# One packed input array for the first loads, and the first two chunks' transposed columns in one transfer each

## The chip, the core and the metric

The kernel runs on one core of a Trainium2 chip. The core has a matrix engine (TensorE, PE in the profile), a vector engine (VectorE, DVE), an activation engine (ScalarE, ACT), a general engine (GpSimd, POOL) and a queue engine (SyncE, SP). PE multiplies from on-chip memory into accumulators; 16 DMA engines bring data from device memory. Each engine works through its own queue in order and waits for others by semaphores. The metric is the time of one execution on the device, in microseconds.

## The reference

Inputs are `x` (1, 2048, 448), `wqkv` (448, 1344), `wo` (448, 448), a gate vector, and the parameters of a state space convolution (448 channels, 256 states). Cut to what matters:

```python
g = sigmoid((x * gate_w).sum(-1, keepdims=True))
# a: linear attention, 16 heads of 28
q, k, v = split_heads(x @ wqkv)
phi = lambda t: where(t > 0, t + 1, exp(t)) + 1e-6
pq, pk = phi(q), phi(k)
kv = einsum("bhsd,bhse->bhde", pk, v);  z = einsum("bhsd->bhd", pk)
num = einsum("bhqd,bhde->bhqe", pq, kv)
den = einsum("bhqd,bhd->bhq", pq, z)[..., None] + 1e-6
a = merge_heads(num / den) @ wo
# b: convolution of x with K over the sequence
P = exp((A * dt[:, None])[:, :, None] * arange(L))
K = 2 * einsum("dn,dnl->dl", C, P).real
b = irfft(rfft(x, 2 * L) * rfft(K, 2 * L))[:L] + x * D_skip
return g * a + (1 - g) * b
```

## The kernel before

The 2048 rows of `x` are cut into 16 chunks of 128. In device memory one array, `xin`, holds for every chunk 128 rows of 1024 numbers (4096 bytes): first 512 numbers of the chunk transposed (four blocks of 128 columns; constants `EV` = 384 and `NAT` = 512 mark the last block's beginning and the end), then 448 in natural order and 64 of them again (`XC` = 1024). The weights for K, Q and V are arrays of 128 partitions by four slices of 448 or 450 columns (`wk_d`, `wq_d`, `wv_d`); a row of one slice is 1792 or 1800 bytes, and rows of one slice lie 7168 or 7200 bytes apart.

Products are made in three parts. Each operand is rounded to a high part (names ending in `h`) and the rest (ending in `l`); PE adds high times high, low times high and high times low. For the x chunks and weight slices at the start, ACT makes the high part (`ACT.copy`, lines 279 and 292) and DVE subtracts (line 269). Only GpSimd makes both parts of the last Q slice.

The order of all work is written out by hand: engines run their queues in program order. At the start chunks 0 and 1 are done together, slice by slice (`pair`, line 561): for K the slices 3, 1, 2, 0, then for Q the same. Slice 3 uses the chunks' columns 384 to 512, the others columns 0 to 384. A slice needs six products of K (two chunks, three parts; the last slice four). The eight K and Q weight slices land in a corner of the output buffer `y` that is free at that time (`wkr`, `wqr`), so the profile shows their loads as `y<-in`; the loads of the chunks are `xr<-in`. Before the first product PE runs eight warm-up products (line 300).

All loads of the start are issued by SP, but for the K slice 3, which ACT issues. They use eight semaphores in turn, so each load waits until the one eight places ahead has landed.

After the two chunks' K and Q, PE goes on with the sums of x-transposed times K features (`do_g`, line 495), then chunk by chunk with K and Q projections (line 396), the convolution's triangular products (line 511), and at the end with transposes of Q features (line 783) and the last product (line 805). Behind the main part stands a branch for a general convolution (`general_conv`), which these inputs don't take.

Of the kernel before, what the change touches and what calls it, by code (L numbers as in the profile page):

```python
# [15 lines left out]
P = 128  # L16
S = 2048
D = 448
# [6 lines left out]
NAT = 4 * P  # L25
LO = NAT + D
XC = LO + 64
# [13 lines left out]
EV = 3 * P  # L41
# [135 lines left out]
            SP.dma_start(out=byc(out, c - ZB + 1), in_=yb)  # L177

@with_exitstack
def gated_mix_kernel(ctx: ExitStack, tc: tile.TileContext, xin, wk_d, wq_d, wv_d, wo_d, abc_d, ldt_d, dsk_d,  # L180
                     tri_d, ident_d, mask_d, gcat_d, sel_d, nabc_d, nldt_d, xrev_d, lag_d, out):
    nc = tc.nc
    PE, ACT, DVE, POOL, SP = nc.tensor, nc.scalar, nc.vector, nc.gpsimd, nc.sync

# [46 lines left out]
    xr, xh, xl = {}, {}, {}  # L231

    def load_x(c):
        xr[c] = pf[:, 4 * D:4 * D + XC] if c == 3 else xp.tile([P, XC], F32, name="xr", tag="xr")
        if c > 1:
            SP.dma_start(out=xr[c], in_=xin[c])

    def load_part(c, lo, hi):
        SP.dma_start(out=xr[c][:, lo:hi], in_=xin[c, :, lo:hi])

    S0 = NC * D - 4 * J * N
    wkr = yf[:, S0:S0 + J * D].rearrange("p (j d) -> p j d", j=J)
    wqr = yf[:, S0 + J * D:S0 + J * (2 * D + 2)].rearrange("p (j d) -> p j d", j=J)
    abc = pf[:DJ, 3 * J * N:7 * J * N].rearrange("p (i j n) -> p i j n", i=4, j=J)
    load_x(0)
    load_x(1)
    for eng, j in ((ACT, 3), (SP, 1), (SP, 2), (SP, 0)):
        if j == 3:
            load_part(0, EV, NAT)
        elif j:  # L250
            load_part(j - 1, 0, EV)
        eng.dma_start(out=wkr[:, j], in_=wk_d[:, j])
        if j == 3:
            load_part(1, EV, NAT)
    for j in (3, 1, 2, 0):
        SP.dma_start(out=wqr[:, j], in_=wq_d[:, j])
    load_part(0, NAT, XC)
    load_part(1, NAT, XC)
    load_x(2)
    SP.dma_start(out=dsk, in_=dsk_d.to_broadcast([P, D]))  # L260
    load_x(3)
# [6 lines left out]
    def low(eng, o, r, h):  # L268
        eng.tensor_tensor(out=o, in0=r, in1=h.bitcast(F32), op=ALU.subtract)  # L269
# [8 lines left out]
    def split_part(c, lo, hi):  # L278
        ACT.copy(xh[c][:, lo:hi], xr[c][:, lo:hi])
        low(DVE, xl[c][:, lo:hi], xr[c][:, lo:hi], xh[c][:, lo:hi])  # L280
# [10 lines left out]
    def high_w(eng, h, r, j):  # L291
        (ACT.copy if eng is ACT else eng.tensor_copy)(h[:, j], r[:, j])

    def low_w(eng, h, l, r, j):
        p = slice(0 if j else 64, P)
        low(eng, (l if j else h)[p, j], r[p, j], h[p, j])
# [256 lines left out]
    def pair(wh, wl, n, tags):  # L553
        o = [ps.tile([P, 512], F32, name=t, tag=t) for t in tags]

        def run(j, parts, last=False):
            xk = slice(j * P, (j + 1) * P)
            for c in range(2):
                for p in parts:
                    a = (xl if p == 1 else xh)[c][:, xk]  # L560
                    PE.matmul(o[c][:, :n], lhsT=a, rhs=(wl if p == 2 else wh)[:, j], start=(j, p) == (3, 0),  # L561
                              stop=last and p == parts[-1])
        return o, run
# [5 lines left out]
    low_w(DVE, wkh, wkl, wkr, 3)  # L569
    split_part(1, EV, NAT)  # L570
    split_part(0, 0, EV)
    high_w(ACT, wkh, wkr, 1)
    low_w(DVE, wkh, wkl, wkr, 1)
    split_part(1, 0, EV)
    kos, k_run = pair(wkh, wkl, D, ("k", "v0"))
    qos, q_run = pair(wqh, wql, D + 2, ("q", "v1"))
    k_run(3, (0, 1, 2))
# [414 lines left out]

_OUT = (S, D)

def _order():
    return [*range(384, D), *range(384)]

def _layout(inputs):
    import numpy as np

    perm = _order()
    x = np.asarray(inputs["A_x"])[0].reshape(NC, P, D)
    inputs = {n: np.asarray(a)[perm] if n[:2] == "B_" and n != "B_u" else a for n, a in inputs.items()}
    xin = np.zeros((NC, P, XC), np.float32)
    xt = x.transpose(0, 2, 1)
    for k in range(3):
        xin[:, :, (k + 1) * P:(k + 2) * P] = xt[:, k * P:(k + 1) * P]
    xin[:, :64, :P] = xt[:, 384:]
    xin[:, 64:, :P] = xt[:, 384:]
    x = x[:, :, perm]  # L1010
    xin[:, :, NAT:LO] = x
    xin[:, :, LO:] = x[:, :, :64]

    def tiles(w):
        o = np.zeros((P, J, w.shape[1]), np.float32)
        for k in range(3):
            o[:, k + 1] = w[k * P:(k + 1) * P]
        o[:64, 0] = w[384:]
        o[64:, 0] = w[384:]
        return o  # L1020

    w = np.asarray(inputs["A_wqkv"])
    wq = np.zeros((D, D + 2), np.float32)
    wq[:, :D] = w[:, :D]
    wq[:, D] = np.asarray(inputs["gate_w"])
    byd = lambda a: np.asarray(a).reshape(J, DJ, -1).transpose(1, 0, 2)
    abc = np.stack([byd(inputs[n]) for n in ("B_log_A_real", "B_A_imag", "B_C_real", "B_C_imag")], axis=1)
    nabc = np.stack([np.asarray(inputs[n]).reshape(GN, GD, 2, P).transpose(0, 3, 2, 1)
                     for n in ("B_log_A_real", "B_A_imag", "B_C_real", "B_C_imag")], axis=2)
    s = np.arange(P)  # L1030
    lag = s[None, :] - s[:, None]
    k = (np.arange(NC)[None, :] - np.arange(NC)[:, None]) * 1.0
    pos = (k > 0) * 1.0
    gc = np.zeros((2, NC - 1, NC, 2))
    gc[0, :, :, 0] = gc[1, :, :, 1] = pos[:-1]
    gc[1, :, :, 0] = (pos * (P * k - 64.0))[:-1]
    gc = np.repeat(gc, 3, axis=3).reshape(NZ, 2, 6 * RG)
    gcat = np.zeros((KZ, 2, RX))
    gcat[:NZ, :, DT:] = gcat[32:, :, DT:] = gc
    sel = np.zeros((P, 2))  # L1040
    sel[:, 0] = s - 63.0
    sel[DT:RX, 1] = -1.0 * (np.arange(RX - DT) % 3 == 1)
    h = np.arange(DJ) // DH
    f = lambda a: np.ascontiguousarray(a, dtype=np.float32)
    return [
        xin,
        tiles(w[:, D:2 * D]),
        tiles(wq),
        tiles(w[:, 2 * D:]),
        f(np.asarray(inputs["A_wo"])[:, perm].reshape(J, DJ, D).transpose(1, 0, 2)),  # L1050
        f(abc),
        f(byd(inputs["B_log_dt"])[:, :, 0]),
        f(np.asarray(inputs["B_D_skip"]).reshape(1, D)),
        f(lag >= 0),
        f(np.eye(P)),
        f(h[:, None] == h[None, :]),
        f(gcat),
        f(sel),
        f(nabc),
        f(np.asarray(inputs["B_log_dt"]).reshape(GN, GD)),  # L1060
        f(x[:, ::-1].transpose(1, 2, 0).reshape(P, GN, GD, NC).transpose(1, 0, 2, 3)),
        f(np.concatenate([np.arange(L1) * L0, np.arange(L0)]).reshape(1, L1 + L0)),
    ]
# [15 lines left out]
```

## Time and profile before

| | |
|---|---|
| median of 3 runs | 185.5 us (184.8, 185.5, 185.63) |
| profiled execution | 184.58 us |
| its span in the profile | 182.7 us |
| granted PE clock | 0.998 |
| busy share of PE, DVE, ACT, POOL | 96%, 74%, 65%, 53% |
| read from device memory, written | 14.25 MB, 3.67 MB |

A busy row of the profile gives an engine's start, duration, line, operation and the tiles it writes and reads; in brackets stands the idle time before it and what ended that. A row of busy time by stage gives for each engine microseconds and number of instructions, then the clock, the mean busy share of the DMA engines and what they moved. KB below are 1024 bytes, kB 1000.

### The profile page before, as it was taken

The numbers are of one execution on the slowest core, as the hardware profiler recorded it, in microseconds if no ns is written. First come the engines' busy times: TensorE is split into PE (matmuls) and PEld (weight loads), VectorE is DVE, ScalarE is ACT, GpSimd is POOL, SyncE is SP. The second block draws the span as 40 slices with busy tenths as digits, with TensorE's granted clock in tenths as the row PEclk, the third lists the DMA queues.
The fourth block names the chain that finished last, engine by engine and source line by source line (L and its number), as shares of the span: only waits on it lengthen the run. The fifth ranks groups of instructions, "written<-read, shape, count | busy, mean of one in ns | idle before, by whom it ended". The sixth has DMA issues, their size and how long they took to land.

```text
span 182.7 us, 2804 instructions
## 1 busy us (share of the span) xinstructions
PE 175.3 (96%) x896; PEld 154.7 (85%) x896; DVE 134.4 (74%) x265; ACT 119.4 (65%) x257; POOL 96.8 (53%) x90
## 2 busy tenths in 40 slices
PE   7799999999999999999999999999999999999990
PEld 7499999998988888898888999889877899899990
DVE  1676298665977799888978878577998698976430
ACT  4699596685756667766687676583665766765530
POOL 1048979752087437164284747039858857864000
PEclk9999999999999999999999999999999999999999
DMA  3999990970021302203031100000001212212222
GB/s 117 320 364 324 245 320 25 382 226 0 0 73 46 115 21 95 88 31 116 9 109 49 74 0 1 6 21 2 2 1 51 105 51 102 101 51 108 100 100 63
DMA packets 8644, 18.34 MB, mean 100 GB/s; under 512 B 1804, under 2 KB 6112, under 8 KB 8400
## 3 DMA queue, kind: packets, MB, share of 16 engines
q1 hardware_dynamic: 8480, 17.88, 29.3%
q10 hardware_dynamic: 144, 0.23, 0.4%
q8 instruction: 9, 0.15, 0.3%
q14 instruction: 11, 0.09, 0.2%
HBM read 14.25 MB, written 3.67 MB: 98 GB/s over the span
## 4 chain that ended last, share of the span: by engine, by line
PE 73%; DVE 11%; ACT 5%; DMA 4%; issue 3%; SPq 1%; POOL 1%; DVEq 0%; ACTq 0%; POOLq 0%
PE a L805 17%; PE g L495 15%; PE q L396 14%; PE k L396 12%; PE v L511 3%; PE tr L783 3%; DMA y<-in 3%; PE v L396 2%; PE v L561 2%; PE q L561 1%; PE k L561 1%; DVE den L739 1%; DVE v L502 1%; DVE th L788 1%; DMA zr<-ru 1%
## 5 line engine op out<-in xcount | busy, mean ns | idle before, releaser
L269 POOL TENSOR_TENSOR xw<-xr,xw 128x448 fp32r<-128x448 f32 (+1 forms) x28 | 34.5, 1250 | 36.7 <-ACT xw L276 24.0
L495 PE MATMUL g<-pkh,xw 128*128 128x448 f32 x112 | 35.5, 366 | 0.0
L396 PE MATMUL q<-wqh,xw 128*128 128x450 f32 x112 | 32.4, 369 | 0.0
L396 PE MATMUL k<-wkh,xw 128*128 128x448 f32 x96 | 27.5, 368 | 0.0
L805 PE MATMUL a<-wkh,th 128*128 128x448 f32 (+1 forms) x119 | 26.9, 365 | 0.0
L734 POOL TENSOR_TENSOR prod<-pq,zb 128x448 f32<-128x448 f32 x16 | 19.2, 1205 | 10.9 <-ACT zb L876 8.3
L495 PE MATMUL g<-pkl,xw 128*128 128x448 f32 x64 | 23.5, 367 | 0.0
L495 PEld LDWEIGHTS g<-pkh,xw 128*128 128x128 f32 x112 | 21.1, 188 | 2.6
L396 PEld LDWEIGHTS q<-wqh,xw 128*128 128x128 f32 x112 | 21.0, 188 | 1.8
L805 PEld LDWEIGHTS a<-wkh,th 128*128 128x128 f32 x119 | 20.7, 190 | 1.3
L755 POOL TENSOR_TENSOR pn<-pq,den 128x448 f32<-128x448 f32 x16 | 15.5, 969 | 8.7 <-DVE den L746 5.0
L396 PEld LDWEIGHTS k<-wkh,xw 128*128 128x128 f32 x96 | 17.9, 188 | 2.0 <-issue 0.3
L283 POOL TENSOR_TENSOR y<-xr,rows 128x448 f32<-128x448 f32 x15 | 17.4, 1163 | 0.0
L396 PE MATMUL q<-wql,xw 128*128 128x450 f32 x42 | 15.4, 368 | 0.0
L810 DVE SCALAR_TENSOR_TENSOR ot<-y,og,a 128x448 f32<-128x448 f32 (+1 forms) x17 | 10.5, 618 | 6.4 <-PE a L805 6.4
L463 ACT ACTIVATE pq<-q 128x448 f32<-128x448 f32 x13 | 7.1, 545 | 12.1 <-DVE q L459 11.0
L417 DVE SCALAR_TENSOR_TENSOR k<-k,e 128x448 f32<-128x448 f32 x13 | 8.2, 632 | 8.9 <-ACT e L414 8.9
L787 ACT CAST th<-tr 128x512 fp32r<-128x512 f32 x16 | 9.4, 587 | 8.1 <-PE tr L783 7.8
L276 ACT CAST xw<-xr 128x1024 fp32r<-128x1024 f32 x13 | 13.6, 1043 | 1.6 <-PE v L511 1.6
L788 DVE TENSOR_TENSOR th<-tr,th 128x512 fp32r<-128x512 f32 x16 | 11.0, 689 | 4.3 <-ACT th L787 4.1
L816 ACT COPY pq<-a 128x448 f32<-128x448 f32 (+1 forms) x17 | 8.7, 514 | 6.8 <-DVE ot L810 6.7
L396 PE MATMUL k<-wkl,xw 128*128 128x448 f32 x36 | 13.2, 366 | 0.0
(182 smaller groups left out, 372.2 us busy)
## 6 DMA issues: line engine op xcount, KB each, us to landing
xr<-in SPq DMA_DIRECT2D x13, 512.0 KB, 4.9
out<-ot SPq DMA_DIRECT2D x15, 224.0 KB, 1.9
pq<-in SPq DMA_DIRECT2D x2, 896.0 KB
y<-in SPq DMA_DIRECT2D x4, 225.0 KB
wv<-in SPq DMA_DIRECT2D x1, 896.0 KB
wo<-in SPq DMA_DIRECT2D x1, 784.0 KB
y<-in SPq DMA_DIRECT2D x3, 224.0 KB, 4.9
xr<-in SPq DMA_DIRECT2D x2, 256.0 KB
```

What stands on the lines that cost most here:

```text
L269: eng.tensor_tensor(out=o, in0=r, in1=h.bitcast(F32), op=ALU.subtract)
L276: ACT.copy(h[:, :XC], r)
L283: POOL.tensor_tensor(out=y[:, c], in0=xr[c][:, NAT:LO], in1=dsk, op=ALU.mult)
L396: PE.matmul(o[:, :n], lhsT=a, rhs=b, start=run.n == 1, stop=not seq)
L495: PE.matmul(g[i][:a.shape[1], :D], lhsT=a, rhs=b, start=c == 0 and n == 0, stop=c == NC - 1 and n == len(seq) - 1)
L734: POOL.tensor_tensor(out=pd[c], in0=pq[:, c], in1=zb, op=ALU.mult)
L755: POOL.tensor_tensor(out=hd(n[:, :D]), in0=hd(pq[:, c]), in1=dn[c // 2][:, c % 2, :, None].to_broadcast([P, H, DH]), op=ALU.mult)
L787: ACT.copy(h, ov)
L788: DVE.tensor_tensor(out=l, in0=ov, in1=h.bitcast(F32), op=ALU.subtract)
L805: PE.matmul(a[:, lo:hi], lhsT=u_, rhs=w_[:, lo:hi], start=n == 0, stop=n == 10)
L810: DVE.scalar_tensor_tensor(out=ot[:, lo:hi], in0=y[:, c, lo:hi], scalar=og[:, c:c + 1], in1=a[:, lo:hi], op0=ALU.mult, op1=ALU.add)
L816: ACT.copy(pq[:, c, lo:hi], a[:, lo:hi])
```

## The change

The first twelve loads come from one new array, `first_d`, in which their contents lie one behind the other in the order of loading, each as a block of 128 rows without gaps. The arrays `wk_d` and `wq_d` fall away; `xin` stays, and its chunks 2 to 15 are loaded from it as before. Of chunks 0 and 1, the 512 transposed columns come as one transfer of 256 KB each, where they came as 64 and 192 KB. ACT still issues K slice 3. The rounding of chunk 1's columns 0 to 384 is put ahead of that of K slice 1.

```diff
-    def load_part(c, lo, hi):
-        SP.dma_start(out=xr[c][:, lo:hi], in_=xin[c, :, lo:hi])
+    at = 0
+
+    def load_first(eng, o):
+        nonlocal at
+        n = P * o.shape[1]
+        eng.dma_start(out=o, in_=first_d[at:at + n].rearrange("(p d) -> p d", p=P))
+        at += n
...
-    for eng, j in ((ACT, 3), (SP, 1), (SP, 2), (SP, 0)):
-        if j == 3:
-            load_part(0, EV, NAT)
-        elif j:
-            load_part(j - 1, 0, EV)
-        eng.dma_start(out=wkr[:, j], in_=wk_d[:, j])
-        if j == 3:
-            load_part(1, EV, NAT)
-    for j in (3, 1, 2, 0):
-        SP.dma_start(out=wqr[:, j], in_=wq_d[:, j])
-    load_part(0, NAT, XC)
-    load_part(1, NAT, XC)
+    for eng, o in first_loads(xr, wkr, wqr):
+        load_first(SP if eng else ACT, o)
...
     split_part(1, EV, NAT)
     split_part(0, 0, EV)
+    split_part(1, 0, EV)
     high_w(ACT, wkh, wkr, 1)
     low_w(DVE, wkh, wkl, wkr, 1)
-    split_part(1, 0, EV)
...
+def first_loads(x, wk, wq):
+    p = [(1, x[0][:, :NAT]), (0, wk[:, 3]), (1, x[1][:, :NAT])]
+    p += [(1, wk[:, j]) for j in (1, 2, 0)] + [(1, wq[:, j]) for j in (3, 1, 2, 0)]
+    return p + [(1, x[c][:, NAT:XC]) for c in range(2)]
...
-        tiles(w[:, D:2 * D]),
-        tiles(wq),
...
+        f(np.concatenate([a.reshape(-1) for _, a in first_loads(xin, tiles(w[:, D:2 * D]), tiles(wq))])),
```

On SP's queue at the start of the program the order was (`xr_104` and `xr_105` are chunks 0 and 1, `in_0` is `xin`, `in_1` and `in_2` the K and Q weights; the shape is partitions by numbers):

```order
L239 DMA xr_104<-in_0 128x128
L239 DMA xr_105<-in_0 128x128
L239 DMA xr_104<-in_0 128x384
L252 DMA y_59<-in_1 128x448
L239 DMA xr_105<-in_0 128x384
L252 DMA y_59<-in_1 128x448 x2
L256 DMA y_59<-in_2 128x450 x4
L239 DMA xr_104<-in_0 128x512
L239 DMA xr_105<-in_0 128x512
```

And it is now (`in_6` is the new array):

```order
L243 DMA xr_104<-in_6 128x512
L243 DMA xr_105<-in_6 128x512
L243 DMA y_59<-in_6 128x448 x3
L243 DMA y_59<-in_6 128x450 x4
L243 DMA xr_104<-in_6 128x512
L243 DMA xr_105<-in_6 128x512
```

The first weight slice on SP (K slice 1) moves from the fourth place to the third, behind both whole 512-column blocks.

On ACT's queue behind the table load and the first small activation, the roundings stood in this order (`xw_146` and `xw_147` are the rounded chunks 0 and 1):

```order
L279 CAST xw_146<-xr_104 128x128
L292 CAST wkh_69<-y_59 128x448
L279 CAST xw_147<-xr_105 128x128
L279 CAST xw_146<-xr_104 128x384
L292 CAST wkh_69<-y_59 128x448
L279 CAST xw_147<-xr_105 128x384
L292 CAST wkh_69<-y_59 128x448 x2
```

and now stand so (`xw_144` and `xw_145` are the same two tiles):

```order
L274 CAST xw_144<-xr_104 128x128
L287 CAST wkh_69<-y_59 128x448
L274 CAST xw_145<-xr_105 128x128
L274 CAST xw_144<-xr_104 128x384
L274 CAST xw_145<-xr_105 128x384
L287 CAST wkh_69<-y_59 128x448 x3
```

K slice 1's rounding moves behind that of chunk 1's 384 columns. The subtractions on DVE's queue move in the same way; PE's and GpSimd's queues keep their order.

More of the change, by code (lines that the diff above doesn't have):

```diff
@@ L179, in gated_mix_kernel @@
 @with_exitstack
-def gated_mix_kernel(ctx: ExitStack, tc: tile.TileContext, xin, wk_d, wq_d, wv_d, wo_d, abc_d, ldt_d, dsk_d,
-                     tri_d, ident_d, mask_d, gcat_d, sel_d, nabc_d, nldt_d, xrev_d, lag_d, out):
+def gated_mix_kernel(ctx: ExitStack, tc: tile.TileContext, xin, wv_d, wo_d, abc_d, ldt_d, dsk_d,
+                     first_d, tri_d, ident_d, mask_d, gcat_d, sel_d, nabc_d, nldt_d, xrev_d, lag_d, out):
     nc = tc.nc
```

## The prediction

> **What bounds the kernel now.** I read the page first, then the chain of waits from the start, then busy time by stage, then the start in detail.
>
> ```profile
> span 182.7 us, 2804 instructions
> PE 175.3 (96%) x896; PEld 154.7 (85%) x896; DVE 134.4 (74%) x265; ACT 119.4 (65%) x257; POOL 96.8 (53%) x90
> ```
>
> TensorE (PE) is busy for 96% of the span. What matters is where it isn't. Busy time in three stages:
>
> ```profile
> core 0: us, PE busy (x) PEld busy (x) DVE busy (x) ACT busy (x) POOL busy (x), PEclk, DMA share, GB/s
> 0.00:7.43 7.43, 5.07 (x23) 4.30 (x23) 2.12 (x7) 3.58 (x8) 0.68 (x5) 1.00 0.59 179
> 7.43:15.61 8.18, 8.18 (x39) 7.08 (x39) 7.07 (x13) 7.78 (x15) 3.62 (x4) 1.00 1.03 372
> 15.61:140.00 124.39, 123.87 (x622) 109.07 (x620) 97.65 (x195) 84.05 (x174) 72.25 (x63) 1.00 0.26 82
> 140.00:182.70 42.70, 38.22 (x215) 34.21 (x215) 27.52 (x54) 23.97 (x63) 20.24 (x20) 0.99 0.24 89
> ```
>
> From 7.43 to 140 us PE idles for 124.39 - 123.87 = 0.52 us in all. So a shift of the moment at which PE's unbroken run begins is carried on almost whole; only that 0.52 us, and waits behind 140 us, could swallow part of it. That moment is 7.43 us, and the chain of waits says what sets it:
>
> ```profile
> 2.17 4.62 DMA y<-in
> 6.79 0.02 issue
> 6.81 0.57 ACT wkh L292
> 7.38 0.04 issue
> 7.43 1.13 PE k L561 x3
> ```
>
> The second K weight slice (call it wk1; wk3 is the first) is issued on SyncE's (SP's) queue at 2.17 and lands 4.62 us later, at 6.79. ScalarE (ACT) rounds it in 0.57 us, and PE starts its products at 7.43. Before that PE has done the six products of wk3, and has idled. So the time of this kernel moves with the arrival of the first loads, and with nothing else that the change touches.
>
> What the DMA engines did in that time, and in a later stage when one x chunk of 512 KB is loaded from idle queues:
>
> ```profile
> 1.70:2.30 0.60, 0.60 (x4) 0.60 (x4) 0.00 (x0) 0.60 (x1) 0.00 (x0) 1.00 0.47 73
> 2.30:3.30 1.00, 1.00 (x7) 1.00 (x6) 0.00 (x0) 0.37 (x2) 0.00 (x0) 1.00 0.90 306
> 3.30:4.30 1.00, 1.00 (x7) 1.00 (x6) 0.10 (x1) 0.43 (x2) 0.00 (x0) 1.00 0.48 139
> 4.30:5.30 1.00, 1.00 (x6) 0.69 (x5) 0.83 (x3) 0.54 (x2) 0.00 (x0) 1.00 0.80 216
> 5.30:6.30 1.00, 1.00 (x5) 0.67 (x4) 0.20 (x1) 0.22 (x1) 0.00 (x0) 1.00 0.89 273
> 6.30:7.30 1.00, 0.13 (x1) 0.00 (x0) 0.56 (x1) 0.78 (x3) 0.00 (x0) 1.00 0.96 308
> 7.30:8.30 1.00, 0.87 (x3) 0.51 (x4) 0.89 (x2) 0.93 (x3) 0.00 (x0) 1.00 1.01 374
> 8.30:9.30 1.00, 1.00 (x6) 0.79 (x6) 0.92 (x3) 0.87 (x3) 0.00 (x0) 1.00 1.06 402
> 9.30:10.30 1.00, 1.00 (x6) 0.91 (x5) 0.97 (x2) 0.93 (x3) 0.00 (x0) 1.00 1.03 393
> ```
>
> ```profile
> 67.12:68.12 1.00, 1.00 (x6) 0.75 (x4) 1.00 (x4) 0.42 (x1) 0.00 (x0) 1.00 0.03 3
> 68.12:68.62 0.50, 0.47 (x3) 0.30 (x2) 0.50 (x2) 0.50 (x2) 0.00 (x0) 1.00 0.71 229
> 68.62:69.12 0.50, 0.50 (x3) 0.28 (x2) 0.20 (x2) 0.50 (x2) 0.00 (x0) 1.00 0.93 344
> 69.12:69.62 0.50, 0.50 (x4) 0.45 (x4) 0.50 (x1) 0.50 (x2) 0.31 (x1) 1.00 0.98 393
> ```
>
> The last column is the point. In the first stretch the queues drop to 139 and 216 GB/s between 3.3 and 5.3 us, although SP has issued seven transfers by 4.03 (below), and reach about 393 only after 7.3. The lone chunk, whose 128 rows lie one behind the other in memory, is at 229, then 344, then 393 within 1 us of its first byte.
>
> **The change, part by part.** *Fewer, larger issues.* The x columns that PE needs turned go from four transfers (64, 64, 192, 192 KB) to two of 256 KB.
>
> ```profile
> 0.76 1.37 SPq L239 DMA_DIRECT2D xr<-in  x3
> 0.76 0.39 ACTq L252 DMA_DIRECT2D y<-in  x1
> 2.17 0.43 SPq L252 DMA_DIRECT2D y<-in  x1
> 2.64 0.43 SPq L239 DMA_DIRECT2D xr<-in  x1
> 3.12 0.91 SPq L252 DMA_DIRECT2D y<-in  x2
> ```
>
> An SP issue comes every 0.47 us (2.17 to 2.64). wk1 was the fourth, now it is the third: issued at about 1.70. The second chunk's whole 256 KB (call it x1) are issued at 1.23 where their larger part was issued at 2.64. Two issues of 0.47 us leave the queue, and nothing is added behind it. Since the transfers then queue at the engines (4.62 us for wk1), this is worth only what it feeds earlier.
>
> *More bytes ahead.* Up to the end of wk1 there were 64 + 64 + 224 + 192 + 224 = 768 KB; now there are 256 + 224 + 256 + 224 = 960 KB. 192 KB (197 kB) at 393 GB/s are 0.50 us, at 273 GB/s 0.72 us. That is the change's price, and it would be paid in full if the transfers ran as before.
>
> The Trainium skill (DMA: Bandwidth & Descriptors, "Issuing engines are not separate DMA queues") says that transfers of all issuers share the same 16 engines and interleave; by it wk3, issued on ACT, no longer shares with two 64 KB pieces but with 256 KB. The rows of 2.30 to 3.30 (306 GB/s with both queues at work) agree that the sum of both, not each, is what counts, and the sum here goes by that total.
>
> *The order on ACT and VectorE (DVE).* ACT now rounds both chunks' larger part before wk1:
>
> ```profile
> 3.87 0.30 ACT L279 CAST xw<-xr 128x128 fp32r<-128x128 f32 x1 [1.20 <-DMA xr<-in]
> 4.08 0.56 ACT L292 CAST wkh<-y 128x448 fp32r<-128x448 f32 x1
> 4.54 0.29 ACT L279 CAST xw<-xr 128x128 fp32r<-128x128 f32 x1
> 6.08 0.51 ACT L279 CAST xw<-xr 128x384 fp32r<-128x384 f32 x1 [1.24 <-DMA xr<-in]
> 6.81 0.56 ACT L292 CAST wkh<-y 128x448 fp32r<-128x448 f32 x1 [0.22 <-DMA y<-in]
> 7.28 0.51 ACT L279 CAST xw<-xr 128x384 fp32r<-128x384 f32 x1
> 7.86 1.26 ACT L292 CAST wkh<-y 128x448 fp32r<-128x448 f32 x2
> 9.06 1.78 ACT L292 CAST wqh<-y 128x450 fp32r<-128x450 f32 x3
> ```
>
> The third cast, of x1's first 128 columns, now waits for all 256 KB of x1, and behind it on ACT's queue stand both 128x384 casts, though chunk 0 has long landed, and then wk1's. A cast starts 0.21 us after a 128-wide one (3.87 to 4.08) and 0.47 after a 448-wide one (6.81 to 7.28); 0.42 for a 384-wide one by proportion. From x1's landing to wk1's cast: 0.02 + 0.21 + 0.42 + 0.42 = 1.07 us; with its 0.57 and the 0.05 to PE (7.38 to 7.43), **PE starts 1.69 us after x1 has landed**, provided that wk1 is there by then. Even at 7.43 as now, x1 must have landed by 5.74. DVE's subtractions follow the same order; its part for wk1 comes behind both 0.55 us subtractions of x, but it had to wait for ACT anyway.
>
> **The main term: when x1 lands.** Through x1 there are 256 + 224 + 256 = 736 KB = 754 kB. No row shows this order, so I bound it.
>
> - Rates of the lone chunk: 44 kB by 2.30 (73 x 0.6), then 0.5 us at 229 and 0.5 at 344 make 331 kB at 3.30; the other 423 kB at 393 end at 4.38.
> - Rates as in the trace of before: 44 + 306 + 139 + 216 = 705 kB at 5.30; the last 49 at 273 end at 5.48.
>
> To this comes the time by which the slowest of the 16 engines is behind the total. Three measures of it: the first 360 kB (64 + 64 + 224 KB) had passed at 3.37, and chunk 0's piece was taken up at 3.87: 0.5 us. In steady flow the third of the casts from 9.06, at about 10.26, took the slice with which 2133 kB were complete, when 44 + 306 + 139 + 216 + 273 + 308 + 374 + 402 + 377 = 2439 had moved: 306 kB, 0.8 us. For wk1, 786 kB were complete at 6.79, 1.2 us after that total had passed (5.60).
>
> So x1 lands between 4.38 + 0.5 = 4.88 and 5.48 + 1.2 = 6.68, and PE starts between 6.57 (0.86 us earlier) and 8.37 (0.94 later). I take the lone chunk's rates, since both x blocks are now of its kind (128 rows, one behind the other, no stride), with the lag of steady flow: 4.38 + 0.8 = 5.18, PE at 6.87, **0.56 us earlier**. wk1 follows 229 kB later, 0.58 us: 5.76, before ACT gets to it at 6.25. wk2 and wk0 follow at the same distance (6.34, 6.92), ahead of casts that come at 6.8 and 7.4.
>
> *What follows.* PE's 38 products to 15.61 run without a break if their inputs keep ahead. The narrowest place is the first G block: its third product needs what GpSimd (POOL) makes from 14.19 on.
>
> ```profile
> 10.91 1.02 POOL L292 CAST wqh<-y 128x450 fp32r<-128x450 f32 x1 [9.68 <-DMA y<-in]
> 14.19 1.16 POOL L269 TENSOR_TENSOR xw<-xr,xw 128x448 fp32r<-128x448 f32 x1 [1.00 <-POOL wqh L269]
> 15.61 0.37 PE L495 MATMUL g<-pkh,xw 128*128 128x448 f32 x1
> ```
>
> It ends at 15.35; the product came two steps of 0.2 us behind 15.61, at about 16.02, so 0.67 us of cover would hold even if POOL's part did not move with the loads. Packing the arrays costs nothing on the chip; the values and PE's 896 matmuls stay.
>
> **Sum.** The profiled execution took 184.58 us, 1.88 around its span of 182.7. 184.58 - 0.56 = 184.0; it lay 0.92 below the median of 185.5, so on that scale 185.5 - 0.56 = 184.94, and I say **185.0**.
>
> **The rivals.** *The layout changes no rate.* If 139 and 216 GB/s come from starting the queues and not from strides, the slow end holds: 192 KB more ahead of wk1, ACT held up behind x1, PE at 8.37: +0.94, 186.4; if the earlier issue of wk1 (1.70 instead of 2.17) is gained in full, +0.47, 186.0. It decides as soon as x1 lands after 5.74. For it: blocks with 7 KB between rows ran at 393 to 402 GB/s after 8 us, so strides alone don't slow a transfer. Against it: the lone contiguous chunk never shows the 139. The Trainium skill (DMA: Bandwidth & Descriptors, "Latency and other measured facts") has a loss from row pitch only at 512 KiB and above, and pitches here are 4 to 7 KB; by that rule this rival would be the outcome. Chance 0.22.
>
> *The start runs at the steady rate.* At 393 from 2.30, 754 kB are through at 2.30 + 710/393 = 4.11, with 0.5 of lag x1 lands at 4.61, PE at 6.30: -1.13, 184.4. For it: 306 GB/s in the second from 2.30 even with half-KB rows. Against: the lone chunk's first half microsecond at 229. Chance 0.2.
>
> *Earlier, but hidden.* PE starts earlier and gives it back at a wait behind 140 us, where it idles 42.70 - 38.22 = 4.48 us on others' work. Then 185.5. Against: those others were themselves released by PE. Chance 0.1.
>
> The forecast (0.1 to 0.9 us earlier, 184.6 to 185.4) keeps 0.48.
>
> **How the numbers follow.** Under 0.5% (0.93 us) a measurement can't tell this kernel from no change: three runs spread over 184.8 to 185.63. Faster by more: the steady-rate case mostly (0.17) and the edge of the forecast with the spread of runs (0.13): 0.30. Slower by more: half of the layout rival, and spread: 0.14. Within: 0.56. The range goes from 184.0 (steady rate, less 0.4 of spread) to 186.3 (the slow end, all but its last tenth); the forecast's own is 184.4 to 185.5.
>
> **What would show it.** The rate from 3.3 to 5.3 us above 300 GB/s instead of 139 and 216; ACT's third cast at about 5.2, waiting for x1; three casts back to back behind it; wk1's cast released by ACT and no longer by its DMA; PE's second slice at 6.9; the first G product at about 15.05. If the rate between 3.3 and 5.3 is as before and that cast comes after 5.74, the layout was not the cause and the change costs time. If PE starts early and the first G product doesn't, a wait between 7 and 15 us has taken the gain.

## The result and the profile after

The changed kernel takes 183.89 us in the median of 14 runs (183.32 to 185.34), the kernel before on the same chip 185.69 us (14 runs, 184.65 to 186.71). The ratio is 0.9926, with a 95% interval of 0.9901 to 0.9950: about 0.7% faster. On the scale of the 185.5 us that were given, this is 185.5 x 0.9926 = 184.1 us. The profiled execution took 183.66 us, with a span of 181.9 where it was 182.7. Medians are over all runs of a kernel; ratios and their intervals leave out executions more than 1.5% above the kernel's fastest.

The page and the busy time by stage, cut where the changed kernel's second K slice and its first G product begin (columns as before):

```profile
span 181.9 us, 2800 instructions
PE 175.4 (96%) x896; PEld 155.1 (85%) x896; DVE 134.7 (74%) x265; ACT 119.1 (65%) x257; POOL 97.0 (53%) x90
```

```profile
core 0: us, PE busy (x) PEld busy (x) DVE busy (x) ACT busy (x) POOL busy (x), PEclk, DMA share, GB/s
0.00:6.90 6.90, 5.36 (x23) 4.55 (x23) 2.31 (x7) 3.89 (x9) 0.68 (x5) 1.00 0.72 241
6.90:15.12 8.22, 8.07 (x40) 7.09 (x39) 7.02 (x13) 7.04 (x14) 3.85 (x4) 1.00 0.98 358
15.12:140.00 124.88, 124.17 (x625) 109.55 (x623) 98.28 (x195) 84.55 (x175) 72.67 (x63) 1.00 0.25 80
140.00:181.90 41.90, 37.84 (x214) 33.90 (x212) 27.11 (x53) 23.62 (x62) 19.83 (x20) 1.00 0.24 90
```

The first G product starts at 15.12 instead of 15.61, 0.49 us earlier. The last group of products starts at 176.47 instead of 176.89, so the shift at the start (0.49) arrives at the end almost whole (0.42). The span is shorter by 0.8; the other 0.4 us of it lie behind the last product, and one profile of each kernel can't say whether that is more than the spread of executions.

The DMA rates at the start:

```profile
2.30:3.30 1.00, 1.00 (x7) 1.00 (x6) 0.00 (x0) 0.36 (x2) 0.00 (x0) 1.00 0.81 292
3.30:4.30 1.00, 1.00 (x7) 1.00 (x7) 0.00 (x0) 0.00 (x0) 0.00 (x0) 1.00 1.09 394
4.30:5.30 1.00, 0.84 (x4) 0.54 (x3) 0.29 (x2) 0.80 (x3) 0.00 (x0) 1.00 1.03 307
```

Where 139 and 216 GB/s stood, there are 394 and 307. The rows of ScalarE (ACT), VectorE (DVE) and TensorE (PE) from the timeline of the changed kernel:

```profile
4.50 0.30 ACT L274 CAST xw<-xr 128x128 fp32r<-128x128 f32 x1 [1.82 <-DMA xr<-in]
4.71 0.56 ACT L287 CAST wkh<-y 128x448 fp32r<-128x448 f32 x1
5.17 1.12 ACT L274 CAST xw<-xr 128x128 fp32r<-128x128 f32 x3
6.20 1.50 ACT L287 CAST wkh<-y 128x448 fp32r<-128x448 f32 x3
...
5.84 1.22 DVE L264 TENSOR_TENSOR xw<-xr,xw 128x128 fp32r<-128x128 f32 x3
6.98 1.16 DVE L264 TENSOR_TENSOR wkl<-y,wkh 128x448 fp32r<-128x448 f32 x2
...
5.32 0.68 PE L556 MATMUL k<-wkh,xw 128*128 128x448 f32 x2 [0.18 <-ACT wkh L287]
6.90 0.60 PE L556 MATMUL k<-wkh,xw 128*128 128x448 f32 x2
7.65 0.47 PE L556 MATMUL k<-wkl,xw 128*128 128x448 f32 x1 [0.15 <-DVE wkl L264]
15.12 0.37 PE L490 MATMUL g<-pkh,xw 128*128 128x448 f32 x1
```

The three casts of x run back to back from 5.17 and wk1's follows them at 6.20 without a gap: ACT's queue releases it, no DMA does. The beginning of its chain of waits says what sets the start now:

```profile
0.76 3.72 DMA xr<-in
4.48 0.02 issue
4.50 0.30 ACT xw L274
4.80 0.48 ACT wkh L287
```

It begins with chunk 0's 256 KB, which land at 4.48, and not with x1: the cast of x1 at 5.17 has no wait before it and stands 0.46 us behind wk3's at 4.71, so x1 had landed by then. Two things are new. The first products start at 5.32, later than before (the first chunk's 256 KB are taken up at 4.50; its first 64 KB were at 3.87), so that the six of them end just as wk1 is rounded. And the third product of wk1 waits for DVE's remainder of wk1, which ends at 6.98 + 0.63 = 7.61: from 6.90 to 7.65 are 0.75 us where two products take 0.41 later in this stage, a loss of 0.34.

### The profile page after: what moved, and what is told of

It is laid out like the page before. It is cut to its first block, busy times and chain, and to the rows that moved or that the text cites. A ratio compares the mean times of both kernels' runs of the same rounds, so it can differ in the third digit from the quotient of the medians.

```text
span 181.9 us, 2800 instructions
## 1 busy us (share of the span) xinstructions
PE 175.4 (96%) x896; PEld 155.1 (85%) x896; DVE 134.7 (74%) x265; ACT 119.1 (65%) x257; POOL 97.0 (53%) x90
## 4 chain that ended last, share of the span: by engine, by line
PE 59%; DVE 15%; issue 11%; ACT 6%; POOL 5%; DMA 2%; POOLq 0%; ACTq 0%
PE a L800 16%; PE g L490 11%; PE q L391 10%; PE k L391 9%; PE tr L778 3%; PE v L391 2%; PE v L506 2%; PE v L556 2%; DVE den L734 2%; DMA xr<-in 2%; DVE v L497 2%; ACT xw L271 2%; POOL xw L264 1%; DVE th L783 1%; DVE wkl L264 1%
```

## Experiments: what removes the dip

The theory on record was that the layout (rows lying one behind the other) lifts the 139 and 216 GB/s. The rivals: the size of the first transfers does, or the new order of rounding is what counts. Two kernels each take half of the change.

**The packed array alone**, with the transfers and the order of before:

```diff
-    p = [(1, x[0][:, :NAT]), (0, wk[:, 3]), (1, x[1][:, :NAT])]
-    p += [(1, wk[:, j]) for j in (1, 2, 0)] + [(1, wq[:, j]) for j in (3, 1, 2, 0)]
+    p = [(1, x[0][:, EV:NAT]), (0, wk[:, 3]), (1, x[1][:, EV:NAT])]
+    p += [(1, x[0][:, :EV]), (1, wk[:, 1]), (1, x[1][:, :EV])]
+    p += [(1, wk[:, j]) for j in (2, 0)] + [(1, wq[:, j]) for j in (3, 1, 2, 0)]
...
-    split_part(1, 0, EV)
     high_w(ACT, wkh, wkr, 1)
     low_w(DVE, wkh, wkl, wkr, 1)
+    split_part(1, 0, EV)
```

> The packed array alone: the twelve-load split with 64 and 192 KB pieces and the order of rounding stay as before. Theory (layout sets the rate): above 300 GB/s between 3.3 and 5.3 us; the slice wk1, 786 kB into the queue, lands near 5.0 us; PE's second slice starts right behind its first, near 6.0, first G product near 14.5; 1.2 to 2 us below the kernel before, 183.7 to 184.5, and no slower than the changed kernel. Rival (fewer and larger transfers make the gain): the dip stays, wk1 near 6.8, second slice near 7.4, time within 0.5 us of before (185.7).

**The larger transfers alone**: 256 KB each and the new order, from the old arrays with gaps between the rows:

```diff
-    for eng, o in first_loads(xr, wkr, wqr):
-        load_first(SP if eng else ACT, o)
+    strided = first_loads([xin[0], xin[1]], wk_d, wq_d)
+    for (eng, o), (_, s) in zip(first_loads(xr, wkr, wqr), strided):
+        (SP if eng else ACT).dma_start(out=o, in_=s)
```

> The two 256 KB transfers and the changed order of rounding, read with stride from the arrays of before. Theory (layout): the rate between 3.3 and 5.3 us stays near 140 to 220 GB/s, the second chunk's 256 KB land at 6.0 to 6.7 us, PE's second slice at 7.7 to 8.4, 0.3 to 0.9 us slower than before (186.0 to 186.6). Rival (larger transfers): above 300 GB/s there, second slice near 6.9, time as the changed kernel (183.9).

**The kernel before once more**, unchanged, for a second profile of it:

> The kernel before, unchanged, profiled once more. Its 14 runs have a median 1.1 us above the profiled one of 184.58 us. Theory (the stride of the first loads makes the start slow, and not always equally): the dip of 139 and 216 GB/s between 3.3 and 5.3 us is there again, PE's second slice starts at 7.4 us or up to 1.5 us later, and the first G product (15.61 before) moves with it by as much as the time does. Rival (the runs differ by something outside the start): second slice within 0.2 us of 7.43, first G product within 0.2 us of 15.61, whatever the time.

Busy time in the two microseconds in question, of the packed array alone:

```profile
3.30:4.30 1.00, 1.00 (x7) 1.00 (x7) 0.01 (x1) 0.34 (x2) 0.00 (x0) 1.00 1.08 192
4.30:5.30 1.00, 1.00 (x5) 0.98 (x5) 0.83 (x2) 0.62 (x2) 0.00 (x0) 1.00 0.64 151
```

of the larger transfers alone (an execution of 186.32 us, the second highest of its 12):

```profile
3.30:4.30 1.00, 1.00 (x7) 1.00 (x7) 0.00 (x0) 0.00 (x0) 0.00 (x0) 1.00 1.04 383
4.30:5.30 1.00, 0.84 (x4) 0.54 (x3) 0.29 (x1) 0.70 (x3) 0.00 (x0) 1.00 1.11 342
```

and of the kernel before in its second profile:

```profile
3.30:4.30 1.00, 1.00 (x7) 1.00 (x7) 0.08 (x1) 0.41 (x2) 0.00 (x0) 1.00 0.51 140
4.30:5.30 1.00, 1.00 (x5) 0.97 (x5) 0.83 (x3) 0.55 (x2) 0.00 (x0) 1.00 0.82 141
```

The theory falls with the first: packing without gaps keeps the dip (192 and 151 GB/s). And 256 KB transfers without packing remove it (383 and 342). In time the packed array alone gives 0.9975 (0.9950 to 1.0001; median 185.42), the larger transfers alone 0.9933 (0.9899 to 0.9967; median 185.12). The difference between the two halves is not beyond their intervals; only the larger transfers' own interval lies clear of 1. A cleaner test of the size is a kernel of the next section that was timed beside these: the packed array with the larger transfers and the order of rounding of before took 183.59 us where the packed array alone took 185.42, and its highest run (184.19) lies below the other's lowest (184.97). The two differ in how the first x loads are cut and ordered, and in nothing else.

The rate is not the whole start, though. In the profile of the larger transfers alone the rounding of the third K slice waits for its load:

```profile
8.05 1.15 ACT L283 CAST wkh<-y 128x448 fp32r<-128x448 f32 x2 [1.19 <-DMA y<-in]
```

Its first G product comes at 15.51, only 0.10 us before the 15.61 of the kernel before; the packed array alone has 15.45. The four profiles with the packing, a large first transfer and the new order have 15.03 to 15.12. But three profiles with the start of before have 15.34, 15.61 and 15.77, so whether gaps between rows delay the later slices can't be told from one profile of a kernel.

Two more kernels narrow it. **Packed weights, x from the old array with gaps** (else as the change):

```diff
-    for eng, o in first_loads(xr, wkr, wqr):
-        load_first(SP if eng else ACT, o)
+    strided = first_loads([xin[0], xin[1]], wk_d, wq_d)
+    for n, ((eng, o), (_, s)) in enumerate(zip(first_loads(xr, wkr, wqr), strided)):
+        if n not in X_AT:
+            load_first(SP if eng else ACT, o)
+        else:
+            SP.dma_start(out=o, in_=s)
...
+X_AT = (0, 2, 10, 11)
```

> The changed kernel with the weights packed and the x columns of the first two chunks read with their stride of 4096 bytes. Theory A (what packing adds comes from the weights, whose rows lay 7 KB apart): time within 0.4 us of the changed kernel, the spread between first and last engine of a weight slice under 0.7 us. Theory B (it comes from x): as the large transfers alone, 0.8 us or more slower than the changed kernel. Both expect above 300 GB/s between 3.3 and 5.3 us.

Measured: 0.9945 (0.9909 to 0.9982, median 184.58), nothing beyond the larger transfers alone, and 0.55 us above the change in the same session (184.03): that lies between its two theories and decides for neither. Its rates were 313 GB/s from 3.3 to 4.3, but 177 from 4.3 to 5.3. It is the one kernel with a large first transfer that shows a dip, a microsecond later, with its first G product at 15.52; the profile is of its slowest run (186.32 us). Here too the x blocks with gaps ran at over 300 GB/s in the first of the two.

**The second chunk's block cut again**, 192 KB before 64 KB, everything packed:

```diff
-    p = [(1, x[0][:, :NAT]), (0, wk[:, 3]), (1, x[1][:, :NAT])]
+    p = [(1, x[0][:, :NAT]), (0, wk[:, 3]), (1, x[1][:, :EV]), (1, x[1][:, EV:NAT])]
```

> The changed kernel with chunk 1's 256 KB in two transfers, 192 KB (rows of 1536 bytes) and 64 KB, behind chunk 0's whole 256 KB. Theory (only a dry queue makes the dip): no dip, above 300 GB/s between 3.3 and 5.3 us, time within 0.4 us of the changed kernel. Rival (rows of 1536 bytes are slow): the rate falls below 250 from about 3.5 us on, PE's second slice at 7.5 or later, 0.5 us or more slower.

Its profile is that of the change: 383 and 312 GB/s, first G product at 15.10, span 182.5. So rows of 1536 bytes and one more issue do no harm to the start of that execution. Its median of 184.95 (ratio 0.9973, 0.9941 to 1.0005) missed what was expected of it: it is 0.92 us above the change in the same session. The profile is of its fastest run (184.28) and can't show what the others lost, so this stays open.

Over all profiles the dip is in every one with two 64 KB pieces at the head (the kernel before twice, the packed array alone, and one more below: 139 and 216, 140 and 141, 192 and 151, 227 and 123 GB/s) and, but for the packed weights, in none of the nine others. What makes it is open. That the engines have run out of work between small transfers is a guess. The DMA share in the rows fits it for the kernel before (0.48 and 0.51 in the first of the two microseconds), but not for the packed array alone, where the engines are counted as busy all through that microsecond (1.08) and move 192 GB/s; the packed weights' 177 speaks against a simple form of it too.

## Experiments: the order of rounding

The change also puts the rounding of the second chunk's 384 columns ahead of wk1's. **The changed kernel with the order of before**:

```diff
     split_part(0, 0, EV)
-    split_part(1, 0, EV)
     high_w(ACT, wkh, wkr, 1)
     low_w(DVE, wkh, wkl, wkr, 1)
+    split_part(1, 0, EV)
```

> The changed kernel with the order of rounding of before (wk1 ahead of the second chunk's 384 columns). Theory (loads set the gain, the order is nearly nothing here): PE's second slice still follows its first without a break near 6.9 us, since wk1 lands at about 5.6; the first G product within 0.2 us of 15.12; time within 0.3 us of the changed kernel (183.9). Rival (the order carries a part of the gain): 0.4 us or more slower than the changed kernel, with a wait of PE in the second slice.

It ran in two sessions, in the second with other expectations:

> The changed kernel with the order of rounding of before, once more beside the others. Measured first: 183.59 where before had 186.15. Expected: 183.3 to 183.8, 0.2 to 0.5 us below the changed kernel's ratio of 0.991 to 0.993, since PE's products of the second slice no longer wait for DVE. Rival (the order makes no difference): a ratio to before of 0.991 to 0.993.

It gave 0.9860 (0.9822 to 0.9898, median 183.59) and 0.9892 (0.9850 to 0.9934, median 183.44). The first session went against both of its theories: the order moves the first G product by more than 0.2 us, and the order of before is the earlier one. Timeline of the second session's profile, DVE and PE:

```profile
6.37 0.62 DVE L264 TENSOR_TENSOR wkl<-y,wkh 128x448 fp32r<-128x448 f32 x1
6.90 0.55 DVE L264 TENSOR_TENSOR xw<-xr,xw 128x384 fp32r<-128x384 f32 x1
...
6.76 0.57 PE L556 MATMUL k<-wkh,xw 128*128 128x448 f32 x2
7.17 0.37 PE L556 MATMUL k<-wkl,xw 128*128 128x448 f32 x1
14.56 0.37 PE L490 MATMUL g<-pkh,xw 128*128 128x448 f32 x1
```

wk1's remainder is ready at 6.37 + 0.62 = 6.99 instead of 7.61, before the product that needs it (7.17), and the first G product comes at 14.56 (14.58 in the first session), 0.56 before the change's 15.12. Of this 0.14 is there at the second slice's start (6.76 for 6.90) and not the order's doing, since chunk 0 was taken up 0.14 earlier in this execution (4.36 for 4.50); 0.34 are the wait that is gone, the rest smaller steps. So most of what the new order costs, 0.34 of 0.42 us, is one wait on DVE. In time the order of before is nominally 0.2 to 0.7% ahead of the change, but the two were never timed in the same session, and all but one pair of their intervals overlap (the change again: 0.9912, 0.9870 to 0.9954, median 184.03).

> The changed kernel once more, beside the experiments. The layout theory has fallen for the rate: packing alone left 192 and 151 GB/s between 3.3 and 5.3 us, large transfers alone gave 383 and 342. New theory: the two 64 KB transfers at the head let the engines run dry at about 3.2 us, and the queue takes 2 us to recover; large ones don't. Packing then adds that no single engine falls behind. Expected: 183.4 to 184.2, 1.5 to 2.5 us below before; rate above 300 between 3.3 and 5.3; PE idle under 0.2 us between 16 and 40 us. Rival (the gain of the first measurement was chance of the runs): 184.5 or more.

The time and the rate came as expected: 184.03 us, 1.72 below the 185.75 of before, with 401 and 362 GB/s. PE idled 0.24 us between 16 and 40 us, a little more than expected.

**A small piece first, then the large one**, packed, with the order of before: 64 KB of chunk 0, 256 KB of chunk 1, then chunk 0's other 192 KB:

```diff
-    p = [(1, x[0][:, :NAT]), (0, wk[:, 3]), (1, x[1][:, :NAT])]
+    p = [(1, x[0][:, EV:NAT]), (0, wk[:, 3]), (1, x[1][:, :NAT]), (1, x[0][:, :EV])]
```

> Packed; the first transfer is the 64 KB of chunk 0 that PE needs first, then at once chunk 1's 256 KB, then chunk 0's other 192 KB (rows of 1536 bytes), then the weights; order of rounding as before. Theory (engines that run dry make the dip): 64 + 224 + 256 KB are at hand by 2.7 us, nothing runs dry, above 300 GB/s between 3.3 and 5.3; PE's first product at 4.7 to 4.9 instead of 5.3, first G product near 14.3, 0.2 to 0.5 us below the changed kernel. Rival (rows of 1536 bytes, or any small first transfer, make the dip): under 250 GB/s there, and at least 0.8 us slower than the changed kernel.

There is no dip (369 and 338 GB/s), the first product comes at 4.68 and the first G product at 14.48, the earliest of all; but the time is 0.9967 (0.9933 to 1.0001, median 184.95), 0.92 us above the change in the same session where 0.2 to 0.5 below was expected. Half of the lead goes at a second gate, which the next section is about, where ACT's rounding of chunk 4 waits for its load:

```profile
26.14 1.05 ACT L271 CAST xw<-xr 128x1024 fp32r<-128x1024 f32 x1 [0.92 <-DMA xr<-in]
```

The first G product is 1.13 us ahead of the first profile of before (14.48 for 15.61); behind that gate PE is 0.53 ahead (the same product starts at 31.48 for 32.01). The profile also has a wait of 1.1 us of PE on DVE near 128 us that the other profiles lack and that takes the rest. That was not followed up: whether it is this kernel's or this execution's is open.

## Experiments: a second gate behind the start

The second profile of the kernel before shows what the first did not. Its first G product comes at 15.77, 0.16 later than in the first profile, yet its span is 185.1, 2.4 us longer: the time was lost outside the start, as the rival of that run had it. Chain of waits (start, duration, what):

```profile
16.73 12.12 DMA xr<-in
28.85 0.02 issue
28.87 1.05 ACT xw L276
29.92 0.45 ACT pkh L425
...
32.77 0.64 DVE pq L457
33.40 0.14 issue
33.54 0.65 PE q L396 x2
```

and in its timeline:

```profile
28.87 1.05 ACT L276 CAST xw<-xr 128x1024 fp32r<-128x1024 f32 x1 [2.36 <-DMA xr<-in]
29.97 0.68 PE L396 MATMUL k<-wkh,xw 128*128 128x448 f32 x2 [0.52 <-ACT xw L276]
33.54 0.65 PE L396 MATMUL q<-wqh,xw 128*128 128x450 f32 x2 [1.04 <-DVE pq L457]
```

Chunk 4 is issued at 16.73 and lands 12.12 us later, with two parameter loads of 896 KB each ahead of it. ACT idles 2.36 us for it at 28.87, and PE pays 0.52 + 1.04 = 1.56 us. In the profile that the prediction was made from, the same cast stands at 26.25 with no wait. What differs besides is the rate of the loads between 15 and 24 us: 284 GB/s there, 236 here, with the same instructions. The two profiles of the change differ in the same way, 298 and 243 GB/s, and only the second waits at this cast (0.79 us). What sets that rate, these runs don't show. The same cast in the changed kernel and in the packed weights':

```profile
25.75 1.03 ACT L271 CAST xw<-xr 128x1024 fp32r<-128x1024 f32 x1
```

```profile
28.69 1.05 ACT L275 CAST xw<-xr 128x1024 fp32r<-128x1024 f32 x1 [2.43 <-DMA xr<-in]
```

In all profiles the span less the start of this cast lies between 155.6 and 157.2 us (182.7 - 26.25 = 156.5; 185.1 - 28.87 = 156.2; 181.9 - 25.75 = 156.2), while the cast itself moves over 3.4 us. That is a correlation; two kernels test it by moving the gate and not the start.

**A useless load of 459 kB behind the first twelve** of the changed kernel, into a part of `y` that is free:

```diff
+    SP.dma_start(out=y[:, 4:6].rearrange("p c d -> p (c d)"), in_=xin[4, :, :2 * D])
```

> The changed kernel with one useless load of 459 kB (1.17 us at 393 GB/s) put behind the first twelve, into rows that are not in use yet. Theory (there is a second gate: the loads form one backlog to about 26 us, and ACT's rounding of chunk 4, for which DVE and PE wait in turn, comes late when chunk 4 lands late): the start is unchanged (first G product within 0.3 us of 15.1), chunk 4's rounding comes at 27 us or later with a wait for its DMA, PE idles 0.8 to 2 us between 16 and 40, and the time rises by 0.6 to 1.4 us over the changed kernel (183.9 to 184.0). Rival (only the start decides): within 0.3 us of the changed kernel.

**The kernel before with 688 kB taken out of the backlog**: of the four parameter arrays, what isn't needed at once is loaded behind chunk 4:

```diff
-    SP.dma_start(out=abc[:, 0:2], in_=abc_d[:, 0:2])
-    SP.dma_start(out=abc[:, 2:4], in_=abc_d[:, 2:4])
+    SP.dma_start(out=abc[:, 0], in_=abc_d[:, 0])
+    SP.dma_start(out=abc[:, 2], in_=abc_d[:, 2])
+    SP.dma_start(out=abc[:, 1:4:2, 0], in_=abc_d[:, 1:4:2, 0])
...
+            SP.dma_start(out=abc[:, 1:4:2, 1:], in_=abc_d[:, 1:4:2, 1:])
```

> The kernel before, with 688 kB of the convolution's parameters that are needed only from about 28 us on loaded behind chunk 4 instead of ahead of it. Nothing else changes, the start least of all. Theory (second gate): chunk 4's rounding never waits, PE idles under 0.2 us between 16 and 40, the time falls by 0.5 to 1.3 us against before and its runs lie closer together. Rival (chunk 4 is late only by accident of a profile): within 0.3 us of before.

Timeline and busy time of the useless load:

```profile
15.03 0.37 PE L491 MATMUL g<-pkh,xw 128*128 128x448 f32 x1
25.08 1.23 DVE L312 TENSOR_REDUCE sp<-pq 112x4 f32<-112x1024 f32 x1 [1.74 <-DMA pq<-in]
26.92 1.05 ACT L272 CAST xw<-xr 128x1024 fp32r<-128x1024 f32 x1 [1.16 <-DMA xr<-in]
16.00:40.00 24.00, 23.39 (x115) 20.95 (x114) 14.00 (x33) 18.39 (x39) 18.50 (x17) 1.00 0.82 244
```

and of the relieved kernel:

```profile
25.97 1.04 ACT L277 CAST xw<-xr 128x1024 fp32r<-128x1024 f32 x1
16.00:40.00 24.00, 24.00 (x119) 21.79 (x118) 15.45 (x34) 18.44 (x40) 19.06 (x18) 1.00 0.88 254
```

With the useless load the start is as good as the change's (15.03), but the chunk comes late, PE idles 24.00 - 23.39 = 0.61 us, and the whole gain is gone: 1.0008 (0.9972 to 1.0045, median 185.47). The direction was as expected, the sizes were not quite: the cast at 26.92 instead of 27 or later, 0.61 us of idle time instead of 0.8 to 2, and a loss of 1.5 to 1.8 us by the ratios (1.0008 for 0.9926 and 0.9912) instead of 0.6 to 1.4. The relieved kernel has the kernel before's first loads, dip included (227 and 123 GB/s), though its first G product comes at 15.34 in this execution; it waits for no chunk 4 and is faster, as expected: 0.9943 (0.9910 to 0.9977, median 184.59), or 0.57% of 185.7 = 1.06 us. Its 12 runs lie within 0.62 us (184.33 to 184.95); the 32 of the kernel before on that chip that its ratio counts spread over 184.57 to 187.31. So most of the spread of the kernel before's runs, and about 1.1 us of its typical run, come from loads between 16 and 29 us. That is the second gate, and it is shown by moving it both ways.

**Both at once**: the order of before on the changed loads, with the same relief:

> Both gates at once: the packed array, the two 256 KB transfers, the order of rounding of before (first G product at 14.6 in its profile), and those 688 kB behind chunk 4. Theory: no wait for chunk 4, and the earlier start is kept to the end: 182.8 to 183.4, 0.3 to 0.8 us below the same kernel without the last edit. Rival (another wait behind 100 us takes the gain): no difference to it.

It came out at 183.91 us (183.63 to 184.78; ratio 0.9910, 0.9880 to 0.9940), missing its expectation. Ten of its 12 runs lie as closely together as the relieved kernel's (183.63 to 184.06), its profile waits for no chunk, and its first G product is at 14.85. But its lowest run is 0.65 us above the lowest of the same kernel without the relief (182.98). The relief takes late executions away and costs something in the good ones, and what that is, these runs don't show. (Its profile is behind from the start: its first product comes at 5.46 for 5.17, where the edit changes nothing.) It beats neither the change nor the order of before by a margin that can be told. From the relieved kernel before (184.59) to it are 0.68 us in the medians (0.49 at the first G product, 14.85 for 15.34), which is what the start is worth once the gate is open.

## Why the prediction was right, and where it was not

- **Direction and time.** 185.0 us with 0.56 us gained was forecast; 184.1 on the same scale was measured, a gain of 1.4 us (0.74%, interval 0.50 to 0.99%). The time is inside the range, the kernel is faster by more than the 0.5% called no change, and the outcome given the largest chance (no change) did not come.
- **The start: the numbers held, the path did not.** PE's second slice was forecast for 6.87 and came at 6.90; the rate was to be above 300 GB/s and was 394 and 307; wk1's cast was released by ACT and not by its DMA; the first G product was forecast for 15.05 and came at 15.12, a gain of 0.49 us for 0.56. But the step "PE starts 1.69 us after x1 has landed" is not what set it. The third cast was to wait for x1 until 5.18; it came at 5.17 without a wait, right behind wk3's. Chunk 0's 256 KB set the start: they were taken up at 4.50 (its first 64 KB at 3.87 before), so the first product came at 5.32, and the second slice began at 6.90 when the six products of the first were done. The prediction had no term for that. That both paths lead to about 6.9 is luck; x1's landing, and with it the lag of 0.8 us, was not measured. (The 0.8 rested on a cast in an unbroken row, whose slice may have landed earlier.) With the gate open (relieved kernel before against the same with changed loads and old order) the start is worth 0.68 us.
- **The cause given for the rate was wrong.** The step "I take the lone chunk's rates, since both x blocks are now of its kind (128 rows, one behind the other, no stride)" had the right numbers for a wrong reason. For the rate from 3.3 to 5.3 us gaps between rows play no measurable part: packing alone left 192 and 151 GB/s and gave 0.9975, larger transfers with the gaps gave 383 and 342. The row of the page that the rival cited (the Trainium skill, DMA: Bandwidth & Descriptors, "Latency and other measured facts") lists losses at row pitches of 512 KiB and more, in copies within device memory, and no smaller pitch. These runs, at 4 to 7 KB, don't contradict it. The prediction let it stand for "no rate changes", and that did not follow: the change had two parts, and the row speaks of one.
- **The order on DVE was costed at nothing.** "Its part for wk1 comes behind both 0.55 us subtractions of x, but it had to wait for ACT anyway" overlooked that PE's third product waits for that part. The wait is 0.34 us in the changed kernel, most of the 0.42 us that the new order costs up to the first G product.
- **The size was too small, and here a step failed**: "the time of this kernel moves with the arrival of the first loads, and with nothing else that the change touches". The loads are one backlog until about 26 us, so a start that gets the queues going sooner can also make chunk 4's landing earlier: by 15 us the two profiles of the change have moved 4.5 and 4.4 MB (302 and 295 GB/s), those of before 4.1 (276 and 271), and chunk 4 is issued at 16.00 instead of 16.49 and 16.73. The profile of before, at 184.58 us, was the lowest of the runs shown and had no wait there. Typical executions are slower (median 185.69; 184.59 in the relieved kernel), and a term for it was missing. Over many runs the kernel before loses about 1.1 us to that gate, by the relieved kernel's ratio. How much of this the change recovers can't be split exactly: its first profile waits 0, its second 0.79 us at the cast, and its ratios (0.9926 and 0.9912 of 185.7: 1.4 and 1.6 us) leave 0.9 to 1.1 us beyond the profile's 0.49 at the start. That these come from the gate is likely and not shown, since the rate between 15 and 24 us differs by as much from one execution to the next.
- **The rivals.** "The layout changes no rate" was right of the rate from 3.3 to 5.3 us, as far as the layout goes, and wrong of the time. The steady rate from 2.3 us on did not come (292 in the first microsecond, then 394). "Earlier, but hidden" did not come for the change. The useless load shows that it can: a start at 15.03 with no gain, given back at 27 to 32 us and not behind 140 as the rival had it.

## What to carry to other kernels

Before a wait is called the only gate, read how much slack each later load of the same backlog has at its landing, and read it in several executions: the runs' spread (2.7 us here, 0.62 with the backlog relieved) says that some wait is there, even if the one profile at hand lacks it. If a change has two parts, ask of each rate which part it rests on, and don't let one rule settle both. And where rounding is reordered for one engine, follow each result to the product that takes it: the high part on ACT was in time here, its remainder on DVE was not.

## What was not expected of the hardware

- Two 64 KB transfers at the head of a program were followed by about two microseconds at 123 to 227 GB/s in four of four profiles, whether or not their rows lay one behind the other. A 256 KB transfer first gave 383 to 401 GB/s in the first and 307 to 362 in the second of them in the change (both profiles), the larger transfers alone and the cut block; the packed weights, with 313 and 177, are the exception.
- The same load on the same kernel (chunk 4, 512 KB behind the same transfers) was rounded at 26.25 without a wait in one execution and at 28.87 after 2.36 us of waiting in another. No instruction differs between the two. Both had the dip at the start (139 and 216, 140 and 141 GB/s); from 15 to 24 us their loads ran at 284 and 236 GB/s.
